# Where the first token tiles are loaded from in a layernorm prologue, and the order of its steps

## The chip, the cores and the metric

One core of a Trainium2 chip runs the kernel. The metric is the device time of one execution in microseconds (us). The kernel before takes 797.77 us, the median of three runs (797.47 to 797.81). Engines are named PE (TensorE), ACT (ScalarE), DVE (VectorE), POOL (GpSimd) and SP (SyncE, which computes nothing and issues transfers). ACT and SP both issue transfers here; such an issue is an instruction in the engine's own queue, which every engine works off in order.

## The reference

```
x  = A_x                      # 2048 tokens x 640, bf16
xn = layernorm(x)             # over the 640, no gain or bias
s  = softmax_attention(xn, wqkv) @ wo        # 32 heads of 20
g  = silu((sigmoid(xn @ w_gate) * (xn @ w_up)) @ w_down)   # 1728 wide
return x + s * g
```

## The kernel before

The 2048 tokens are 16 tiles of 128 tokens ("x0" to "x15"), each 128x640 bf16 or 160 KB. A prologue loads them, normalizes and transposes them, and computes keys, values and the first queries of the first heads. After it, a long main phase runs attention and the gated block, with its order written out by a planner at build time. The change touches the prologue alone.

**Loads.** Line 215 issues the 16 loads before any computing: x1 and x3 from ACT's queue, the other fourteen from SP's. Behind x7 come two loads of the first head group's weights (`wst`, line 127), behind x15 one load `wv` (line 139).

**Steps of a tile.** `s_stats` is mean and variance: on DVE two `bn_stats` and a `bn_aggr` (lines 270, 271), on ACT two activations with a sum (lines 275, 276; tiles 2, 5, 7, 11, 12 and 15). `s_rstd` on POOL (lines 280 to 285) takes two tiles at a time. Then `s_xn` on DVE (line 291), `s_tr` (five transposes on PE, line 298, into one of four `tp` buffers) and `s_ev` (copy out, DVE or ACT, line 301). For each chunk of four tiles follow `s_k` (key matmuls, line 318), `s_kt` (key copy, ACT, line 324), `s_kmax` (line 329); for the first chunks `s_v` and `s_vev` (values), and for the first `s_q`, `s_abs`, `s_bound`, `s_qev` (first queries). `s_table` is a tiny exponential (line 227 calls line 85) that brings in ACT's function table early.

**Order.** The steps form a graph of `Step` objects, each with an assumed duration per engine, an earliest time `at`, and a lateness weight (`L_...`, `EARLY`). A loop (lines 436 to 454) walks an assumed clock in steps of 0.02 us and gives each free engine the most urgent step that its assumed times allow; where PE has nothing it issues a `scrap` matmul on ones (line 451), so that PE stays busy. The loop only fixes the order in which instructions stand in each engine's queue. On the chip each waits for its real inputs. `X_AT` is the loop's assumed arrival of each x tile.

```
SP  L215 xt_114 (x7)
SP  L127 wst           waits DMAHW0   (x0)
SP  L127 wst           waits DMAHW1   (x1)
SP  L215 xt_115 (x8)   waits DMAHW2   (x2)
ACT L215 xt_108 (x1), xt_110 (x3)     no waits
```

## Time and profile before

| | |
|---|---|
| runs | 797.47, 797.77, 797.81 us |
| profiled execution | 797.83 us, of which the span of instructions is 795.6 us |
| granted clock | 0.999 |
| busy over the span | PE 97%, DVE 97%, ACT 98%, POOL 13% |
| first scores of the main phase (line 956) | start at 26.85 us |

Times in the text are microseconds from the start of the span. A row of the timeline gives start, duration, engine, line, operation, and in brackets the idle time of the engine before it with what ended it. "SPq" and "ACTq" are the transfer issues on those engines.

### The profile page before, as it was taken

The numbers are of one execution on the slowest core, as the hardware profiler recorded it, in microseconds if no ns is written. First come the engines' busy times: TensorE is split into PE (matmuls) and PEld (weight loads), VectorE is DVE, ScalarE is ACT, GpSimd is POOL, SyncE is SP. The second block draws the span as 40 slices with busy tenths as digits, with TensorE's granted clock in tenths as the row PEclk, the third lists the DMA queues.
The fourth block names the chain that finished last, engine by engine and source line by source line (L and its number), as shares of the span: only waits on it lengthen the run. The fifth ranks groups of instructions, "written<-read, shape, count | busy, mean of one in ns | idle before, by whom it ended". The sixth has DMA issues, their size and how long they took to land.

```text
span 795.6 us, 24034 instructions
## 1 busy us (share of the span) xinstructions
PE 771.1 (97%) x9799; PEld 264.0 (33%) x9803; DVE 770.0 (97%) x1243; ACT 779.6 (98%) x980; POOL 100.7 (13%) x200
## 2 busy tenths in 40 slices
PE   8999999999999999999999999999999999999997
PEld 6523222333233233333223332333333233332332
DVE  8899999999999999999999999999999989999997
ACT  8899999999999999999999999999999999999995
POOL 7100000000100001000010000000000000321421
PEclk9999999999999999999999999999999999999999
DMA  5632212223232133223133323233123222231221
GB/s 164 188 79 51 67 46 58 58 69 82 63 81 66 41 88 104 51 55 76 44 63 86 80 54 85 75 108 109 37 61 85 66 69 53 70 110 41 69 65 54
DMA packets 107461, 59.06 MB, mean 74 GB/s; under 512 B 53579, under 2 KB 102779, under 8 KB 107351
## 3 DMA queue, kind: packets, MB, share of 16 engines
q1 hardware_dynamic: 106647, 56.98, 27.8%
q8 instruction: 76, 1.25, 0.7%
q10 hardware_dynamic: 704, 0.56, 0.2%
q14 instruction: 34, 0.28, 0.1%
HBM read 43.21 MB, written 9.13 MB: 66 GB/s over the span
## 4 chain that ended last, share of the span: by engine, by line
ACT 56%; PE 21%; DVE 13%; issue 9%; DMA 1%; DVEq 0%; ACTq 0%
ACT pt L85 44%; PE bk L526 8%; PE scA L956 7%; ACT px L85 7%; DVE iv L1399 5%; PE oacc L993 4%; ACT tnh L85 4%; DVE pb L1101 2%; DVE pb L1095 1%; ACT td L85 1%; DVE pb L1098 1%; DVE stats L270 1%; DVE hT L743 1%; ACT aq L176 0%; DMA xt<-in_A_x_dram 0%
## 5 line engine op out<-in xcount | busy, mean ns | idle before, releaser
L85 ACT ACTIVATE pt<-scA 128x1024 bf16<-128x1024 f32 x707 | 699.9, 1172 | 0.4
L1399 DVE TENSOR_SCALAR iv<-bk 128x512 int16<-128x512 f32 x500 | 331.5, 680 | 10.2 <-PE bk L956 8.2
L956 PE MATMUL scA<-q,kT 32*128 32x512 bf16 x1407 | 274.9, 382 | 11.6 <-ACT pt L85 7.0
L956 PE MATMUL bk<-q,kT 32*128 32x512 bf16 x641 | 203.6, 383 | 0.2
L993 PE MATMUL oacc<-pt,v 128*21 128x512 bf16 x1407 | 185.4, 382 | 1.0 <-ACT pt L85 1.0
L956 PEld LDWEIGHTS <-kT 32*128 32x128 bf16 x2048 | 86.3, 91 | 287.4 <-issue 277.5
L993 PE MATMUL oacc<-pb,v 128*21 128x512 bf16 x1000 | 161.2, 382 | 0.1
L526 PE MATMUL bk<-xnT,wgu 128*32 128x512 bf16 x2160 | 159.2, 383 | 0.8
L1101 DVE TENSOR_TENSOR pb<-iv,pb 128x2048 bf16<-128x2048 bf16 (+1 forms) x126 | 152.7, 1212 | 0.8
L1049 POOL TENSOR_TENSOR on_bf<-on,rl 128x128 bf16<-128x128 f32 x116 | 56.4, 492 | 636.0 <-DVE pb L1101 186.1
L85 ACT ACTIVATE px<-bk 128x512 bf16<-128x512 f32 x141 | 102.6, 741 | 0.9 <-PE bk L956 0.9
L1095 DVE TENSOR_SCALAR pb<-iv 128x2048 int16<-128x2048 int16 (+1 forms) x126 | 85.8, 681 | 0.7
L1098 DVE TENSOR_SCALAR pb<-iv 128x2048 int16<-128x2048 int16 (+1 forms) x126 | 85.7, 680 | 0.0
L526 PE MATMUL bk<-hT,wd 128*32 128x512 bf16 x1120 | 82.6, 384 | 0.5 <-DVE hT L754 0.2
L993 PEld LDWEIGHTS <-v 128*21 128x21 bf16 x2548 | 52.6, 91 | 80.8 <-issue 58.8
L526 PEld LDWEIGHTS <-wgu 128*32 128x32 bf16 x2160 | 44.9, 95 | 62.0 <-issue 43.4
L526 PE MATMUL bk<-xnT,wu 128*32 128x512 bf16 x640 | 48.6, 383 | 0.2 <-DVE iv L1399 0.2
L993 PE MATMUL oacc<-px,v 128*21 128x512 bf16 x141 | 48.0, 382 | 0.0
L85 ACT ACTIVATE tnh<-bk 128x512 bf16<-128x512 f32 (+1 forms) x56 | 41.7, 745 | 0.1
L743 DVE SCALAR_TENSOR_TENSOR hT<-tnh,bk 128x512 bf16<-128x512 bf16 x52 | 35.3, 679 | 0.5 <-PE bk L526 0.2
L526 PEld LDWEIGHTS <-wd 128*32 128x32 bf16 x1120 | 20.5, 95 | 33.5 <-issue 27.1
L707 PE MATMUL bk<-wv,xnT 128*128 128x160 bf16 x280 | 28.0, 234 | 0.8 <-ACT px L85 0.6
(128 smaller groups left out, 397.4 us busy)
## 6 DMA issues: line engine op xcount, KB each, us to landing
rl<-rd SPq DMA_DIRECT2D x124, 64.0 KB
wgu<-in_B_w_gate_dram SPq DMA_DIRECT2D x24, 320.0 KB
wgu<-in_B_w_up_dram SPq DMA_DIRECT2D x24, 320.0 KB
xnT<-in_A_x_dram SPq DMA_DIRECT2D x16, 160.0 KB
xt<-in_A_x_dram SPq DMA_DIRECT2D x14, 160.0 KB
oU<-on_bf SPq DMA_DIRECT2D x108, 20.0 KB
wd<-in_B_w_down_dram SPq DMA_DIRECT2D x1, 2080.0 KB
out_dram<-xnT SPq DMA_DIRECT2D x13, 160.0 KB
```

What stands on the lines that cost most here:

```text
L85: return nc.scalar.add_instruction(mybir.InstActivation(func=func, name=nc.get_next_instruction_name(), engine=ENG.Activation, ins=[nc.sca ...
L270: nc.vector.bn_stats(out=stats[:, h, :], in_=xts[k][:, h * HD:(h + 1) * HD])
L526: nc.tensor.matmul(out[j:j + 32, :], lhsT=lhsT[:, j:j + 32], rhs=rhs, start=start, stop=stop, tile_position=(0, j), skip_group_check=True)
L707: nc.tensor.matmul(st["ps"][:, i * 2 * GC:(i + 1) * 2 * GC], lhsT=xn_tok(tts[i], kd), rhs=wvs[pr][:, kd, :], start=(kd == 0), stop=(kd == ...
L743: return nc.vector.scalar_tensor_tensor(out=hT[0:fs, kf, :], in0=st["t"][0:fs, :], scalar=1.0, in1=st["u"][0:fs, :], op0=ALU.add, op1=ALU. ...
L956: nc.tensor.matmul(dst, lhsT=kTs[gc_of(b)[0] % 2][32 * j:32 * j + 32, kt * P:(kt + 1) * P], rhs=qts[b % 3][32 * j:32 * j + 32, :], start=T ...
L993: nc.tensor.matmul(oacc[32 * j:32 * j + DH + 1, :], lhsT=lhsT, rhs=u["src"], start=first, stop=last, tile_position=(0, 32 * j), skip_group ...
L1049: ins = nc.gpsimd.tensor_tensor(out=on_bf[:, cs], in0=on[:, cs], in1=rl[:, cs], op=ALU.mult)
L1095: ins = nc.vector.tensor_scalar(out=pb[:, 0, :, :].bitcast(I16), in0=iv, scalar1=0x7F80, scalar2=1, op0=ALU.bitwise_and, op1=ALU.bitwise_or)
L1098: ins = nc.vector.tensor_scalar(out=pb[:, 1, :, :].bitcast(I16), in0=iv, scalar1=0x007F, scalar2=0x3F00, op0=ALU.bitwise_and, op1=ALU.bitw ...
L1101: ins = nc.vector.tensor_tensor(out=pb[:, 1, :, :], in0=iv.bitcast(BF16), in1=pb[:, 1, :, :], op=ALU.mult)
L1399: beat(nc.vector.tensor_scalar(out=d["iv"][:, j, :], in0=bank[bk], scalar1=B_OFF, scalar2=0.0, op0=ALU.add, op1=ALU.max))
```

## The change

x0, x1 and x2 now come from SP. The loads of x3 and x6 move to ACT, and no longer stand with the other loads: they are issued in the step `s_table`, behind the table load, and that step runs inside the loop, after all of SP's loads have been written down. In the loop `s_table` is allowed 2.9 us from 0.3. `X_AT` and several weights are new, which reorders some steps. No computation is added or taken out.

```diff
-    X_AT = (3.2, 3.4, 3.8, 4.3, 4.7, 5.2, 5.8, 6.4, 8.9, ...
+    X_AT = (3.2, 3.7, 4.2, 4.5, 4.8, 5.3, 5.5, 6.0, 8.4, ...
-    L_ST, L_CH, L_K, L_V, L_Q = 2.0, 1.5, 6.5, 9.5, 1.5
-    L_QH, L_QL, L_KT, L_KM, L_TR, L_EV = 14.5, 10.0, 2.0, 7.0, -4.0, 0.0
+    L_ST, L_CH, L_K, L_V, L_Q = 2.0, 1.5, 7.5, 9.5, 1.5
+    L_QH, L_QL, L_KT, L_KM, L_TR, L_EV = 14.5, 10.0, 2.0, 8.0, -8.0, 0.0
-    EARLY = {('stats', 14): 4.0, ('stats', 11): -2.0, ('ev', 9): -2.0, ('xn', 1): 8.0}
+    EARLY = {('stats', 14): 4.0, ('stats', 11): -2.0, ('xn', 1): 8.0, ('ev', 5): -2.0, ('xn', 15): 2.0, ('tr', 15): 8.0, ('tr', 9): 8.0}
+    ACT_LOADS = (3, 6)
...
         for k in range(TT):
-            (nc.scalar if k in (1, 3) else nc.sync).dma_start(out=xts[k], in_=x2[k * P:(k + 1) * P, :])
+            if k not in ACT_LOADS:
+                nc.sync.dma_start(out=xts[k], in_=x2[k * P:(k + 1) * P, :])
             if k == 7:
                 wst0 = load_wst(0)
         wv0 = load_wv(0)
...
         def s_table(eng):
             exp_act(eps_t, eps_t)
+            for k in ACT_LOADS:
+                nc.scalar.dma_start(out=xts[k], in_=x2[k * P:(k + 1) * P, :])
...
-        table = Step(s_table, (), {"ACT": 1.3}, at=1.3)
+        table = Step(s_table, (), {"ACT": 2.9}, at=0.3)
```

The built program of the changed kernel begins so on the two queues that issue transfers (line numbers are those of the changed file; the tile's number is added):

```
SP  L217 xt_107 (x0), xt_108 (x1), xt_109 (x2), xt_111 (x4), xt_112 (x5), xt_114 (x7)    no waits
SP  L127 wst, wst                                    no waits
SP  L217 xt_115 (x8)       waits DMAHW0
SP  L217 xt_116 (x9)       waits DMAHW1
SP  L217 xt_117 (x10)      waits DMAHW2
SP  L217 xt_118 (x11)      waits DMAHW3
...
ACT LoadActFuncSet
ACT L85  Activation eps_t
ACT L229 xt_110 (x3)       waits DMAHW0, until it has counted two transfers
ACT L229 xt_113 (x6)       waits DMAHW2, until it has counted two transfers
ACT L279 Activation sq (statistics of x2)
```

Past the prologue the order of instructions is the same on every engine. Within it, these steps stand elsewhere: on DVE the statistics of tile 14 ahead of those of tile 8, the `xn` of tile 15 ahead of the statistics of tile 13, `ev` of tile 15 ahead of the first `kmax`; on PE a scrap matmul between the transposes of tiles 7 and 10, the transposes of tile 15 ahead of those of tile 11, the last key matmuls of 256 columns into a `tp` buffer ahead of the transposes of tile 12; on ACT the first `abs` behind two copies, the second `kt` behind `ev` of tile 9, the narrow `kt` ahead of `ev` of tile 12. POOL's order is the same.

More of the change, by code (lines that the diff above doesn't have):

```diff
@@ L203 @@
     RH = 2
-    X_AT = (3.2, 3.4, 3.8, 4.3, 4.7, 5.2, 5.8, 6.4, 8.9, 9.4, 9.9, 10.4, 11.0, 11.5, 12.0, 12.6)
-    L_ST, L_CH, L_K, L_V, L_Q = 2.0, 1.5, 6.5, 9.5, 1.5
-    L_QH, L_QL, L_KT, L_KM, L_TR, L_EV = 14.5, 10.0, 2.0, 7.0, -4.0, 0.0
+    X_AT = (3.2, 3.7, 4.2, 4.5, 4.8, 5.3, 5.5, 6.0, 8.4, 8.9, 9.4, 9.9, 10.4, 10.9, 11.4, 12.0)
+    L_ST, L_CH, L_K, L_V, L_Q = 2.0, 1.5, 7.5, 9.5, 1.5
+    L_QH, L_QL, L_KT, L_KM, L_TR, L_EV = 14.5, 10.0, 2.0, 8.0, -8.0, 0.0
     KSB = (1, 1, 1, 0, 1)
-    EARLY = {('stats', 14): 4.0, ('stats', 11): -2.0, ('ev', 9): -2.0, ('xn', 1): 8.0}
+    EARLY = {('stats', 14): 4.0, ('stats', 11): -2.0, ('xn', 1): 8.0, ('ev', 5): -2.0, ('xn', 15): 2.0, ('tr', 15): 8.0, ('tr', 9): 8.0}
+    ACT_LOADS = (3, 6)
     ACT_STATS = (2, 5, 7, 11, 12, 15)
```

## The prediction

> **What bounds the kernel now.** First the page: three engines are nearly full, so time lost ahead of the main phase is not won back there.

> ```profile
> PE 771.1 (97%) x9799; PEld 264.0 (33%) x9803; DVE 770.0 (97%) x1243; ACT 779.6 (98%) x980; POOL 100.7 (13%) x200
> ```

> Then the chain of waits of the first 30 us, which opens with the load of x0 and runs on DVE:

> ```profile
> 0.80 3.03 DMA xt<-in_A_x_dram
> 3.86 0.90 DVE stats L270 x2
> 4.78 0.21 DVE mv L271
> 4.99 0.76 DVE stats L270 x2
> 5.77 0.21 DVE mv L271
> 5.98 0.76 DVE stats L270 x2
> ```

> Third, busy time by stretches. The columns are length, then PE, PEld, DVE, ACT, POOL:

> ```profile
> 4.00:10.00 6.00, 3.96 (x34) 2.84 (x32) 5.83 (x19) 5.19 (x13) 5.38 (x13) 1.00 0.97 289
> 10.00:16.00 6.00, 5.88 (x63) 4.63 (x62) 5.86 (x18) 5.90 (x14) 5.03 (x15) 1.00 0.60 145
> 16.00:22.00 6.00, 5.62 (x64) 4.19 (x63) 5.97 (x17) 5.95 (x13) 2.32 (x7) 1.00 0.00 1
> 22.00:25.00 3.00, 3.00 (x37) 2.53 (x36) 2.92 (x9) 2.07 (x4) 0.00 (x0) 1.00 0.00 0
> ```

> DVE is busy 20.58 of these 21 us: what delays it early in its queue delays the first scores (26.85) in full. Fourth, the timelines of the two issuing queues, ACT first:

> ```profile
> 0.80 0.88 ACTq L215 DMA_DIRECT2D xt<-in_A_x_dram  x2
> 1.71 1.28 ACT L85 ACT_TABLE_LOAD   x1 [1.71 <-PEq L1587]
> 4.72 0.74 ACT L275 ACTIVATE sq<-xt 128x640 bf16<-128x640 bf16 x1 [1.51 <-DMA xt<-in_A_x_dram]
> ```

> ```profile
> 0.80 2.80 SPq L215 DMA_DIRECT2D xt<-in_A_x_dram  x6
> 3.85 0.96 SPq L127 DMA_DIRECT2D wst<-in_A_wqkv_dram  x2
> 4.86 3.95 SPq L215 DMA_DIRECT2D xt<-in_A_x_dram  x8
> ```

> SP's first six issues end at 3.60, but the seventh starts only at 3.85, when x0 has landed (the trace has its semaphore full at 3.84). SP's waits name that gap:

> ```profile
> SPq L127 <- DMA xt<-in_A_x_dram: 0.2, 1, 0.2
> ```

> So the semaphore that a transfer shares with the one eight before it holds back its issue, and the queue behind it. That decides this change.

> **The waits that the change adds.** In program order x3 and x6 now come behind SP's loads. x3 shares its semaphore with x0 and x8 and is issued only when x8 has landed; x6 shares with x2 and x10 and waits for x10. Both waits stand on ACT ahead of its first statistics. Behind x3's issue are queued x6's issue, the statistics of x2, x5, x7 and all later ACT work; DVE's third item, the statistics of x3, waits for the landing. Before, x3 was issued at 1.23 and used at 5.90.

> **When x8 lands.** SP's issues take 2.80/6 = 0.467 us: x0, x1, x2, x4, x5, x7 from 0.80 to 3.60. The `wst` pair has fresh semaphores now and follows at once (0.96), so x8 is issued at 4.6; its own wait, for x0, is then over (x0 landed 3.03 after issue). From issue to landing: x0 3.03, x2 3.45 (1.27 to 4.72), x8 3.8 (4.86 to 8.65, by the trace's semaphores). The last had two more tiles ahead; landings of x5, x6 and x7 are 0.43 apart on average (6.37, 6.83, 7.23), so without them 3.8 - 0.86 = 2.9. I take 3.1, between the unloaded and the loaded rows: x8 lands at 7.7, ends 7.5 and 8.4.

> **When x3 lands.** Issued at 7.7. On ACT's queue x1 took 2.83 (0.80 to 3.63) and x3 3.28 (1.23 to 4.51). I take 2.9, nearer x1, since nothing stands ahead of it on its queue: 10.6, ends 10.3 and 11.85. DVE's statistics of x3 start at 10.6 instead of 5.90: **+4.7** (4.4 to 5.95).

> **ACT beside it.** x10 is issued two SP issues behind x8 (3.95/8 = 0.49 each, 0.55 behind the weights), about 5.7, and lands 3.2 later at 8.9. Then x6's issue (0.43) frees ACT at 9.35 instead of 4.72: +4.6. This lies beside DVE's +4.7; if x3 came early, ACT's delay would be the bound. x6 lands near 11.8, DVE wants it at 8.19 + 4.7 = 12.9: covered by 1.1, and past that it costs its lateness one for one.

> **x0, x1, x2 from SP.** x0 no longer shares its first microsecond with x1 and may land up to 0.4 earlier; that only moves DVE's statistics of x0 and x1 ahead of the new stall, so 0. x1 and x2, issued at 1.27 and 1.73, land by about 5 and are wanted at 4.9 and 9.35; a lateness of x1 falls into the same stall. The table load starts at about 0.85 instead of 1.71, hidden by the wait for x8: 0.

> **New order.** Instruction counts per engine are the same, so the price is only in waits. `xn` of tile 15 (0.39) ahead of the statistics of tile 13 delays POOL's `rstd` for tile 12 by 0.36 (it ended at 21.26, `xn` of tile 12 started at 21.36); `ev` of tile 15, moved ahead of `kmax`, delays that `xn` by 0.40 too, which keeps the cover at 0.1. The second `kt` goes behind a 0.58 copy, which puts its release of the key bank level with PE's next key matmuls. PE's transposes of tile 15, moved forward, have their `xn` some 0.5 earlier. Sum 0 to +0.2; I take 0. A gain is bounded by the whole slack of DVE, 21 - 20.58 = 0.4.

> **PE's rate after the stall.** PE ends its first 28 scraps at 6.43 and waits for the first `xn`, at 8.34:

> ```profile
> 1.31 5.12 PE L451 MATMUL scrap<-busy 128*128 128x256 bf16 x28 [1.31 <-DVE busy L430]
> 8.34 0.45 PE L298 MATMUL tp<-ident,xn 128*128 128x128 bf16 x5 [1.90 <-DVE xn L291]
> 8.62 0.93 PE L451 MATMUL scrap<-busy 128*128 128x256 bf16 x7
> ```

> 28 scraps in 5.12 us against 7 in 0.93: in the trace the first start 213 ns apart, those from 5.4 on 109 ns. PE started at half rate and took 3.9 us of work to leave it; 1.9 us of idling did not bring it back. (The page's clock column shows 1.00 throughout.) Now the first `xn` moves to 8.34 + 4.7 = 13.0, an idle of 6.6 us that no row has. The nearest rows are full rate after 1.9 idle and half rate at the start. I take half rate: 6.6 is over three times the idle shown harmless. Its cost: from the first transposes to `ev` of tile 3 on DVE, PE has 20 transposes of 55 ns and 8 scraps of 109 ns, 1.97 us, which become 3.94. Slack there is 0.41 idle ahead of 9.69, and 0.41 between the transposes of tile 3 (end 10.88) and DVE's `ev` (11.29). So +1.97 - 0.82 = **+1.2** (0 at full rate; 2.4 if it lasts into `q` and `k`, whose 1.2 us of doubling the later 0.34 idle hardly covers).

> [...]

> **Sum.** 4.7 + 0 + 1.2 = 5.9 on the profiled execution's 797.83 (span 795.6 and 2.2 around it; the median is 0.06 below): **803.7 us**. All later loads, the second `wst` too, move along with the work that frees their buffers.

> **Rivals.** (a) *The clock stays.* Everything as above with PE at full rate: 797.83 + 4.7 = 802.5. For it: 109 ns right after 1.9 us idle. Against: the start.

> (b) *Not slower: the issues do not wait.* If ACT sends both loads on at once, x3 goes out at 2.15 (0.85 + 1.28) and lands 2.9 later at 5.1, ahead of 5.90; x6 lands at 5.5, ahead of 8.19. Then only x0's up to 0.4 remains and DVE gains at most that: 797.4 to 797.8. It decides if x8 has landed by 5.9 - 2.9 = 3.0, or if the wait binds nobody. Against: x8 cannot be issued before 4.6, and SP's gap to 3.85 shows such a wait binding. It is also the case where the change does what its words say.

> [...]

> (c) *Longer.* x8 lands at 8.4, x3 takes 3.45, PE stays at half rate into `q` and `k`: 5.95 + 2.4 = 8.35, 806.2. For it: x8's 3.8 and x2's 3.45 before.

> **Numbers.** Forecast 0.60, (a) 0.22, (b) 0.06, (c) 0.12. The range leaves out (b) and most of (c): its low end is (a) with x3's early end, 797.83 + 4.4 = 802.2, less 0.4 for DVE's slack: 801.8. Its high end is x3's late end with +1.2, near 805.0, and 0.4 of the longer half rate: 805.4. A measurement of this kernel tells 0.2% (1.6 us) from no change. Faster by more: 0.01, (b) with a gain that its price doesn't hold; within: 0.05; slower: 0.94.

> **What would show it.** ACT's queue after: table load at 0.85, x3's issue near 7.7, x6's near 8.9, first statistics near 9.35. DVE: a second wait for a load, about 5 us, ended by x3 near 10.6. PE: scraps after 13.0 at 213 ns instead of 109. First scores near 32.7. It is wrong if x3's issue stands near 2.1, if DVE's wait is under 4 us, or if the first scores move by something other than DVE's wait plus PE's loss.

## The result, and the profile after

The changed kernel takes 806.02 us (median of 4 runs, 805.3 to 806.68); the kernel before, beside it, 797.79 (797.47 to 798.25). The ratio is 1.0103, 95% interval 1.0085 to 1.012: 8.2 us slower. The forecast was 803.7 with a range to 805.4, so the direction was right and the size too small.

The profiled execution took 805.3 us, its span 803.4 (before 795.6). The page's first section shows nearly the same busy time in a longer span:

```profile
PE 771.9 (96%) x9803; PEld 264.2 (33%) x9803; DVE 770.0 (96%) x1243; ACT 780.0 (97%) x980; POOL 99.6 (12%) x200
```

The chain of the first 37 us (start, length, what) now goes over SP's issues up to 4.66 and then over two transfers, one behind the other:

```profile
4.66 4.54 DMA xt<-in_A_x_dram
9.22 3.75 DMA xt<-in_A_x_dram
13.00 0.90 DVE stats L274 x2
...
15.48 0.71 PE tp L302 x5
16.20 1.49 PE scrap L455 x7
...
19.01 0.49 DVE xnT L305
...
34.60 0.39 PE scA L960 x2
```

The first is x8, from its issue to its landing, and the second x3. The first scores start at 34.60 instead of 26.85. That is +7.75, and the span grew by 7.8: all of the loss lies ahead of the main phase.

ACT's timeline shows the wait standing ahead of its first statistics:

```profile
0.80 1.28 ACT L85 ACT_TABLE_LOAD   x1 [0.80 <-PEq L1591]
9.22 1.16 ACTq L229 DMA_DIRECT2D xt<-in_A_x_dram  x2
10.42 0.74 ACT L279 ACTIVATE sq<-xt 128x640 bf16<-128x640 bf16 x1 [8.13 <-DMA xt<-in_A_x_dram]
```

SP's timeline has lost its gap ahead of the weights, and x8 goes out at 4.66 (4.86 before):

```profile
0.80 2.77 SPq L217 DMA_DIRECT2D xt<-in_A_x_dram  x6
3.62 1.00 SPq L127 DMA_DIRECT2D wst<-in_A_wqkv_dram  x2
4.66 4.45 SPq L217 DMA_DIRECT2D xt<-in_A_x_dram  x8
```

DVE's timeline: the first two tiles come early, then DVE idles 7.72 us for x3, whose statistics stood at 5.90 before.

```profile
3.15 0.89 DVE L274 BATCH_NORM_STATS2 stats<-xt 128x6 f32<-128x320 bf16 x2 [1.89 <-DMA xt<-in_A_x_dram]
4.20 0.83 DVE L274 BATCH_NORM_STATS2 stats<-xt 128x6 f32<-128x320 bf16 x2
13.00 0.89 DVE L274 BATCH_NORM_STATS2 stats<-xt 128x6 f32<-128x320 bf16 x2 [7.72 <-DMA xt<-in_A_x_dram]
```

Busy time by stretches (length, PE, PEld, DVE, ACT, POOL, then clock, DMA share and GB/s): DVE has 1.21 busy us of six in the first stretch, where it had 5.83.

```profile
4.00:10.00 6.00, 2.14 (x17) 1.54 (x15) 1.21 (x5) 0.00 (x0) 3.11 (x7) 1.00 0.91 264
10.00:16.00 6.00, 0.52 (x6) 0.52 (x7) 2.94 (x9) 5.03 (x12) 1.48 (x4) 0.62 0.51 151
```

PE's timeline: idle 9.35 us, then 7 scraps in 1.70 us where the same 7 took 0.93.

```profile
15.48 0.71 PE L302 MATMUL tp<-ident,xn 128*128 128x128 bf16 x5 [9.35 <-DVE xn L295]
15.99 1.70 PE L455 MATMUL scrap<-busy 128*128 128x256 bf16 x7
```

From these rows the loss splits in two. The statistics of x3 start at 13.00 instead of 5.90: **+7.1**. From there to the first scores it takes 21.60 us instead of 20.95: **+0.65**.

### The profile page after: what moved, and what is told of

It reads as the page before. It is cut to its first block, busy times and chain, and to the rows that moved or that the text cites. A ratio compares the mean times of both kernels' runs of the same rounds, so it can differ in the third digit from the quotient of the medians.

```text
span 803.4 us, 24037 instructions
## 1 busy us (share of the span) xinstructions
PE 771.9 (96%) x9803; PEld 264.2 (33%) x9803; DVE 770.0 (96%) x1243; ACT 780.0 (97%) x980; POOL 99.6 (12%) x200
## 4 chain that ended last, share of the span: by engine, by line
ACT 55%; PE 21%; DVE 13%; issue 9%; DMA 1%; SPq 0%; DVEq 0%; ACTq 0%
ACT pt L85 44%; PE bk L530 8%; ACT px L85 7%; PE scA L960 6%; DVE iv L1403 5%; PE oacc L997 4%; ACT tnh L85 4%; DVE pb L1105 2%; DVE pb L1099 1%; DVE pb L1102 1%; ACT td L85 1%; DMA xt<-in_A_x_dram 1%; DVE hT L747 1%; PE tp L302 1%; DVE stats L274 0%
## 5 line engine op out<-in xcount | busy, mean ns | idle before, releaser
L85 ACT ACTIVATE pt<-scA 128x1024 bf16<-128x1024 f32 x707 | 699.8, 1171 | 0.4
L1403 DVE TENSOR_SCALAR iv<-bk 128x512 int16<-128x512 f32 x500 | 331.2, 680 | 10.4 <-PE bk L960 8.5
L960 PE MATMUL scA<-q,kT 32*128 32x512 bf16 x1407 | 274.9, 382 | 11.5 <-ACT pt L85 7.0
L85 ACT ACTIVATE px<-bk 128x512 bf16<-128x512 f32 x141 | 102.6, 741 | 0.9 <-PE bk L960 0.9
L85 ACT ACTIVATE tnh<-bk 128x512 bf16<-128x512 f32 (+1 forms) x56 | 41.6, 743 | 0.1
L530 PEld LDWEIGHTS <-wd 128*32 128x32 bf16 x1120 | 20.5, 95 | 33.5 <-issue 27.1
```

What stands on the lines that cost most here:

```text
L85: return nc.scalar.add_instruction(mybir.InstActivation(func=func, name=nc.get_next_instruction_name(), engine=ENG.Activation, ins=[nc.sca ...
L530: nc.tensor.matmul(out[j:j + 32, :], lhsT=lhsT[:, j:j + 32], rhs=rhs, start=start, stop=stop, tile_position=(0, j), skip_group_check=True)
L960: nc.tensor.matmul(dst, lhsT=kTs[gc_of(b)[0] % 2][32 * j:32 * j + 32, kt * P:(kt + 1) * P], rhs=qts[b % 3][32 * j:32 * j + 32, :], start=T ...
L1403: beat(nc.vector.tensor_scalar(out=d["iv"][:, j, :], in0=bank[bk], scalar1=B_OFF, scalar2=0.0, op0=ALU.add, op1=ALU.max))
```

## The experiments

Theory A, which all the expectations start from: the late landing of x3 stops DVE, and it is late because its issue waits for the landing of x8; a smaller part is PE's half clock after the idle. The rivals put the cost on the block on ACT, on the new order of steps, or on the second queue. Later runs ask why the two landings came later than forecast. The diffs are against the changed kernel unless it says otherwise.

### The loads written at their place

x3 and x6 stay on ACT, behind an early table load, but stand among the other loads, so that their semaphores are fresh.

```diff
+        nc.vector.memset(eps_t, 0.0)
+        exp_act(eps_t, eps_t)
         for k in range(TT):
-            if k not in ACT_LOADS:
-                nc.sync.dma_start(out=xts[k], in_=x2[k * P:(k + 1) * P, :])
+            (nc.scalar if k in ACT_LOADS else nc.sync).dma_start(out=xts[k], in_=x2[k * P:(k + 1) * P, :])
...
         def s_table(eng):
-            exp_act(eps_t, eps_t)
-            for k in ACT_LOADS:
-                nc.scalar.dma_start(out=xts[k], in_=x2[k * P:(k + 1) * P, :])
+            pass
...
-        nc.vector.memset(eps_t, 0.0)
```

> The changed kernel with the loads of x3 and x6 written down at their place among the other loads (still ScalarE's queue, still behind the table load, new step order kept). The built program then gives neither a wait. Theory A (the issues wait for the landing of x8 and x10, eight transfers back on a shared semaphore): both go out by about 3 us, statistics of x3 start near 5.2 to 5.9, first scores near 26.9, total 797.6 to 798.2, ratio to before 1.000 +- 0.0006. Rival B (loads from ScalarE behind the table load are slow by themselves): x3 still lands several us later than 5.9, total above 801. Rival C (the new step order costs it): total near 806, since the order is kept.

Measured: 798.51 us (797.89 to 799.09, 10 runs), ratio to before 1.001 (1.0001 to 1.002). First scores at 27.6. ACT's timeline of this run:

```profile
0.80 1.28 ACT L85 ACT_TABLE_LOAD   x1 [0.80 <-PEq L1589]
0.97 0.86 ACTq L218 DMA_DIRECT2D xt<-in_A_x_dram  x2
5.29 0.74 ACT L278 ACTIVATE sq<-xt 128x640 bf16<-128x640 bf16 x1 [3.00 <-DMA xt<-in_A_x_dram]
```

Same queue, same transfers, same order of steps, only without the late partner to wait for: 7.3 of the 8.2 us are gone. The time is 0.3 above theory A's range, and 0.9 above the kernel before beside it (797.61). The chain of waits of this run goes over the landing of x5 and on over ACT's statistics:

```profile
3.23 4.06 DMA xt<-in_A_x_dram
7.32 0.84 ACT sq L278 x2
```

Before, x5's statistics started at 6.40. In this build one weight load also stands earlier, x8 is issued at 5.29 (4.86 before), and x2's statistics start at 5.29 (4.72 before). So the 0.9 goes with loads that land later on ACT's side; which part of the new distribution makes them later was not separated.

### The order alone, and the loads alone

First the kernel before with only `X_AT`, the weights and the table step's assumed time of the change; then the changed kernel with all of these put back.

> The kernel before with the new assumed arrivals, weights and step order, loads as before (x1 and x3 from ScalarE ahead of the table load). Theory A: the order by itself costs 0 to 0.2 us, total 797.6 to 798.1. Rival C: total 803 or more.

> The changed kernel's loads (x3 and x6 in the step with the table load) with the step order of before. Theory A: the same two waits, so the same delay as the changed kernel: statistics of x3 start at 12.5 to 13.5, first scores near 34.5, total 805 to 806.5. Rival C: total near 798.

Measured: order alone 797.54 (797.05 to 797.87, 10 runs), ratio 0.9998 (0.9988 to 1.0007), first scores at 27.0; loads alone 805.89 (805.14 to 806.1, 4 runs), ratio 1.0101 (1.0086 to 1.0116). The order costs nothing that can be measured, and the loads carry the whole loss. The chain of waits of the loads alone is a second sample of the same two transfers, x8 and x3: x8 takes less and x3 more, and the end (12.95) is the same to 0.02.

```profile
4.67 3.95 DMA xt<-in_A_x_dram
8.64 4.31 DMA xt<-in_A_x_dram
```

### The same late loads from SP

```diff
         wv0 = load_wv(0)
+        for k in ACT_LOADS:
+            nc.sync.dma_start(out=xts[k], in_=x2[k * P:(k + 1) * P, :])
...
-            for k in ACT_LOADS:
-                nc.scalar.dma_start(out=xts[k], in_=x2[k * P:(k + 1) * P, :])
```

> The changed kernel with the loads of x3 and x6 issued from SyncE, as the last behind x15 and wv, instead of from ScalarE; ScalarE's queue then holds no wait and does its statistics from about 4.7 on. x3 is issued near 9.7 (behind the landing of x9) and lands near 13.3 to 13.9. Theory A (the late data of x3 on VectorE sets the end, ScalarE's own blocked queue lies beside it): no gain, 806.0 to 807.0. Rival D (the blocked ScalarE queue is what costs): total 803 or less, although x3 is as late.

Measured: 806.44 (806.21 to 807.25, 4 runs), ratio 1.0108 (1.0091 to 1.0125). ACT starts its statistics at 4.73, nearly as before, and it brings nothing. SP's timeline of this run shows the two late issues:

```profile
9.16 1.00 SPq L222 DMA_DIRECT2D xt<-in_A_x_dram  x2
```

DVE's timeline shows that the statistics of x3 still wait for them:

```profile
13.14 0.89 DVE L274 BATCH_NORM_STATS2 stats<-xt 128x6 f32<-128x320 bf16 x2 [7.92 <-DMA xt<-in_A_x_dram]
```

The block on ACT is not the cost here; the late data are. Rival D falls.

### Only x3 at its place

x3 goes back among the loads as in the first experiment; x6 stays in `s_table`. In this build one weight load stands behind x2.

> Only x3 goes back to its place among the loads (from ACT's queue, behind an early table load; it waits for nothing). x6 stays in s_table, and its issue waits on ACT for the landing of x8, so ACT is still blocked. Theory A (DVE's wait for late data is the cost; ACT's block counts only once x3 is early): x8 is issued near 4.9 and lands 3.4 to 4.5 later, ACT is free near 9.0 to 9.9, x6 lands near 12 to 13.2. DVE has the statistics of x0, x1, x3, x4 early and then stops for x6 or for what ACT's statistics of x2 release: first scores 4 to 6 later than before, 802 to 804. Rival B (the block on ACT is covered by DVE's other work, only x3 counts): within 1.5 of 798.5. Rival C (ACT's block costs by itself as much as x3's lateness): 805 to 806.7, as the changed kernel.

Measured: 804.24 (six of 7 runs at 802.4 to 804.75, one at 811.32), ratio 1.0094 (1.0065 to 1.0122), the profiled run 802.4. The chain of waits of this run again has two transfers in a row, now x8 and x6, and DVE stops for x6:

```profile
4.71 3.78 DMA xt<-in_A_x_dram
8.51 3.86 DMA xt<-in_A_x_dram
12.39 0.90 DVE stats L276 x2
```

First scores at 31.8, 5.0 later than before; theory A's 4 to 6 holds in the profile, and the median is just past its 804. In the changed kernel x6's lateness was hidden behind x3's: x6 landed at 13.65 (by the trace's semaphores), and DVE came to its statistics only at 15.34. So both loads cost, but not in sum: mending one of them only shows the other.

### PE kept busy

Eighty more `scrap` matmuls on ones ahead of the first transposes, on PE alone.

```diff
+        for _ in range(80):
+            nc.tensor.matmul(scrap[:, 0:2 * P], lhsT=busy[:, 0:P], rhs=busy, start=True, stop=True)
```

> The changed kernel with 80 more scrap matmuls ahead of the first transposes, so that TensorE works until about 15 us instead of 6.13 and the first transposes (15.48) find it busy just before. Theory A with the clock as a part (TensorE idles 9.35 us in the changed kernel, falls to half rate, which costs 0.6 us between the statistics of x3 and the copy of tile 3 on VectorE: 6.01 us apart instead of 5.39 before): the two are 5.4 apart again, granted clock 1.00 from 13 to 19 us, total 0.6 us below the changed kernel, 805.0 to 805.8. Rival (the half rate is hidden, the 0.6 is something else): still 6.0 apart, total unchanged near 806.

Measured: 804.53 (804.4 to 805.38, 4 runs), ratio 1.0087 (1.0072 to 1.0102). The clock column stays at 1.00, and from the statistics of x3 (12.54) to the first scores (33.53) it takes 20.99 us, as before the change (20.95; 21.60 with the change). The 0.65 was the clock. The time fell by 1.5, more than the expected 0.6: x3 landed 0.46 earlier in this run's profile, and other runs of the changed kernel seem to have been longer at half clock than its profiled one (PE's clock, in the next section).

### Where the landings' time comes from

Four runs shift what is in flight beside the two transfers. First the weights (`wst`) behind x15:

> The changed kernel with the two loads of the first head group's weights (rows of 160 bytes) moved behind x15 on SyncE. x3 still waits for x8 and x6 for x10, but x8 is now issued near 3.6 instead of 4.66 and nothing with small rows lies ahead of it. In the changed kernel x8 took 4.56 us from issue to landing where 3.1 was forecast. Theory A1 (the small rows ahead made x8 late): x8 lands about 3.1 after issue, x3 is issued near 6.8 and its statistics start near 10.3, total 802.8 to 803.8. Rival A2 (one transfer engine among the sixteen happens to lag, whatever lies ahead): x8 takes 4 to 4.6 again, x3 is issued at 7.7 to 8.2, statistics of x3 near 11.7, total 804.2 to 805.2. Rival B and C: unchanged, near 806.

Then half the columns of the tiles ahead of x8 (x1, x2, x4, x5, x7), or of those behind it (x9 to x15). These kernels leave out part of the input: the other columns of these tiles are set to zero on DVE, further down in the edit.

```diff
+    HALF = (1, 2, 4, 5, 7)          # or range(9, TT)
...
-                nc.sync.dma_start(out=xts[k], in_=x2[k * P:(k + 1) * P, :])
+                w = HD if k in HALF else D
+                nc.sync.dma_start(out=xts[k][:, 0:w], in_=x2[k * P:(k + 1) * P, 0:w])
```

> The changed kernel, but of x1, x2, x4, x5 and x7 only the first 320 columns are loaded and the rest is set to zero by VectorE: half the bytes ahead of x8, as many transfers and rows. Part of the input is left out. In the changed kernel x8 took 4.56 us from issue to landing, with the small-row weights moved away 4.15. Theory A1 (bytes ahead on the same queue make x8 late): 3.0 to 3.4, x3 issued by 8.1. Rival A2 (the count of rows, or single transfer engines that lag): 3.8 to 4.6, x3 issued at 8.5 to 9.3. Total follows x3's issue one for one, 804.5 to 806.5.

> The changed kernel, but of x9 to x15 only the first 320 columns are loaded and the rest is set to zero by VectorE: half the bytes that run beside x3's load. Part of the input is left out. In the changed kernel x3 took 3.75 us from issue to landing, against 2.83 and 3.28 on the same queue before. Theory A3 (SyncE's loads beside it take the bandwidth): 2.8 to 3.3. Rival A4 (ScalarE's queue or single lagging transfer engines, whatever runs beside): 3.6 to 4.3. x8's landing should not move (9.2 +- 0.6). Total 804.8 to 806.5.

And both halves at once:

> The changed kernel with only the first 320 of 640 columns loaded of x1, x2, x4, x5, x7 and of x9 to x15 (the rest is set to zero): half the bytes ahead of x8 and half beside and behind it; x0, x3, x6 and x8 are whole. Theory A (both landings were forecast too early because the queued bytes of other loads stretch them; with less of them the forecast's own 3.1 and 2.9 come back): x8 lands 2.8 to 3.2 after its issue at 4.65, x3 is issued near 7.5 to 7.9 and lands 2.8 to 3.2 later, 10.4 to 11.0 (forecast 10.6). First scores 21.6 to 22.5 later, 32.0 to 33.5; time 802.9 to 804.3. Rival B (the two halves relieve the same thing, so that the second adds nothing to the first): x3 lands at 11.0 to 11.5, time 804.6 to 805.2.

All of it in one table, from the chains and timelines: from x8's issue to its landing, from x3's issue to its landing, start of DVE's statistics of x3, and the time with its ratio to before.

| kernel | x8 | x3 | stats x3 | time, ratio (interval) |
|---|---|---|---|---|
| forecast | 3.1 | 2.9 | 10.6 | 803.7 |
| changed | 4.54 | 3.75 | 13.00 | 806.02, 1.0103 (1.0085 to 1.012) |
| loads alone | 3.95 | 4.31 | 12.97 | 805.89, 1.0101 (1.0086 to 1.0116) |
| PE busy | 3.82 | 4.01 | 12.54 | 804.53, 1.0087 (1.0072 to 1.0102) |
| late loads from SP | 4.05 | 3.96 | 13.14 | 806.44, 1.0108 (1.0091 to 1.0125) |
| weights last | 4.13 | 3.71 | 11.50 | 804.44, 1.0083 (1.0068 to 1.0098) |
| half ahead | 3.36 | 4.64 | 12.71 | 805.53, 1.0097 (1.0077 to 1.0117) |
| half behind | 3.20 | 3.16 | 11.07 | 804.83, 1.0088 (1.0068 to 1.0109) |
| half of both | 2.76 | 3.48 | 10.96 | 803.88, 1.0079 (1.0061 to 1.0097) |

Each row but the forecast is one profile. Putting the weights last lets x8 out at 3.62 instead of 4.66, and that is its gain; the 4.13 lies within the 3.82 to 4.54 of the other runs with full loads, where A1 expected 3.1, so the small rows ahead were not what made x8 late. A2's numbers fit, but no run shows a single engine that lags. Half the bytes ahead take x8 to 3.36, as A1 expected; x3's 4.64 in that run, the longest of all, was not expected and stays open. Half the bytes *behind* take x8 to 3.20, although none of these was issued before it and the expectation had its landing unmoved, and they take x3, which is issued on another queue, to 3.16. So in these runs a landing depends on what is in flight beside it, issued before or after, on either queue. The two runs with less behind x8 also had fewer of the stalled packets that the last section shows, two and one against six to fourteen in the rows with full loads; for them the runs cannot tell fewer bytes from fewer stalls. x3 took 3.96 from SP's queue in one profile, and 3.75 to 4.31 from ACT's in the three others with the same loads: no difference between the queues shows here.

With both halves x3's statistics start at 10.96 (forecast 10.6) and the kernel takes 803.88: in time, the forecast described a queue with half the load, though x8 took less than its 3.1 and x3 more than its 2.9. x3's 3.48 is 0.3 over theory A's bound for its own part. In time and at x3's landing the run sides with theory A; x3 alone took a little longer than with the later half only, so the two halves do not simply add.

## Why the prediction was right or wrong

**The waits bind: right.** x3's issue stands right behind x8's landing (9.20 by the trace's semaphores, issue at 9.22); the trace has x0, x8 and x3 on one semaphore, with 16 counts each, the last at 3.12, 9.20 and 12.97. ACT's queue waits with it and DVE stops for x3. Rival (b) is out, and the first experiment shows that the partner alone makes the wait.

**When x8 lands: the first step that failed.** The forecast took x8's 3.8 of before, subtracted 0.86 for two tiles that no longer stood ahead, and settled on 3.1, with 3.8 as its late end. It measured 4.54, and 3.82 to 4.05 in the three other runs with the same loads up to there: the subtraction bought nothing. One of the two tiles was no load on x8 even before: x3 had landed at 4.51, and x8 went out at 4.86. The 3.8 was also a single sample; the order-only run, which has the loads of before, gives 4.13 (4.80 to 8.93, by the trace's semaphores). And the step priced only what stands ahead, while the seven tiles issued behind x8, the same before and after, weigh as much by the half-behind run. Why the absence of the other tile, x6, bought nothing either stays open. Term: +1.5.

**When x3 lands: the second.** The 2.9 came from x1, loaded at 0.80 with little in flight, with the reason that nothing stands ahead of x3 on ACT's queue. At 9.22 all seven tiles behind x8 were still in flight (they landed from 9.59 to 12.21), `wv` followed at 9.61, and x3 took 3.75 (3.71 to 4.64 in the runs with full loads behind it). Rival (c)'s 3.45 was too short as well. Term: +0.85. The two make 2.35 of the 2.4 by which DVE's stall, +7.1 instead of +4.7, was too small.

**ACT beside it: right in kind.** ACT was free at 10.42 (forecast 9.35), because x10 landed at 10.02 instead of 8.9, and it stayed beside the path. That x6 costs its lateness once it is no longer covered is what the run with only x3 at its place shows. The forecast also said that with x3 early ACT's delay would be the bound; this did not come about: in that run ACT began its statistics only at 8.92, but DVE stopped for x6's data.

**x0 to x2, the table, the order: right.** x0 lands 0.7 earlier (the forecast said at most 0.4), which only moves DVE's first two items ahead of the stall. The table load is hidden. The order alone is 0.9998 of before.

**PE's clock: right that it falls, and the size depends on the execution.** Half rate after the long idle was the forecast's estimate from two rows of before. The profile shows half clock and 0.65 instead of 1.2. The slack that the forecast took off was read a little too large: of its 0.41 ahead of 9.69, 0.11 is the last scrap's own time (it starts at 9.28), which leaves 0.30. In the loads-alone profile the same stretch (statistics of x3 to first scores) takes 22.13 us, +1.18. That profiled run took 806.1, the changed kernel's 805.3. The changed kernel's other runs have no trace, but their granted clock is on record: 0.993, 0.992 and 0.994, against 0.996 in the profiled one. Four profiles with 6.83 us of half clock show 0.995 to 0.996, four with 10.24 us show 0.992 to 0.993 (the last section has these lengths). So two of the three read like the longer half clock; the one at 0.994 lies between.

**Sum.** 7.1 + 0.65 = 7.75 against 4.7 + 1.2 = 5.9. With the longer half clock it is 7.1 + 1.18 = 8.3, near the 8.2 of the medians. Rival (c) came within 0.2 us of the median by luck, with another split: 5.95 of stall, which is too little, and 2.4 of clock, which is too much. The range ended too low because both its ends for the landings came from single rows of before, while four profiles of the same loads spread over 0.7 us for x8 and, on either queue, 0.6 for x3.

## What to carry to other kernels

Before moving a transfer in the program, count which one its semaphore is shared with: here a load moved from the fourth to the seventeenth place of the program waited for the ninth to land, and two transfers in a row stood on the path ahead of DVE where one, x0, had. Write a load that is needed early among the first ones, whatever queue issues it (798.51 us here with both loads in place on ACT's queue, 806.02 with them late there, 806.44 late on SP's). And price a transfer on a full queue with what is in flight beside it, behind it and on other queues too, and with the spread of several samples rather than one row: x8 took 3.20 us with half the bytes behind it, and 2.76 to 4.54 over the profiles here.

## What the runs showed of the hardware

**Half clock lasted 6.83 or 10.24 us.** PE's clock column in half-microsecond windows (length, busy PE, clock, DMA share, GB/s) places its fall and its return, of the changed kernel:

```profile
11.00:11.50 0.50, 0.00 (x0) 0.94 0.89 271
18.00:18.50 0.50, 0.50 (x9) 0.73 0.00 0
```

and of the loads alone:

```profile
9.00:9.50 0.50, 0.00 (x0) 0.93 0.91 236
19.50:20.00 0.50, 0.50 (x5) 0.83 1.15 185
```

The windows between read 0.50 in both, and so a value of 0.94 in a window of 0.5 us stands for half clock in its last 0.06 us. The clock fell at 11.44 and came back at 18.27 in the first, 9.43 and 19.67 in the second: 6.83 and 10.24 us. In all eight profiles in which it fell ahead of the main phase, the clock records show one of these two lengths. The fall came 5.3 us after the last scrap in the one and 2.6 in the other; with only x3 at its place it came 1.3 after (scraps to 9.43, fall at 10.73), sooner than the 1.9 of idling that the prediction read as harmless. So the length of the idle alone does not say when the clock falls, and what does was not shown. From the statistics of x3 to the first scores it took 0.65 longer than before in the changed kernel's profile, with 6.83 us of half clock, and 1.18 longer in the loads-alone one, with 10.24.

**Single packets stall.** In the packet records of the first 13 us a 1280-byte packet takes 0.055 us (median), but a few take 0.5 to 1.27. In the changed kernel one lasts from 7.67 to 8.81; the second weight load lands at 8.77, 1.77 behind the first, and x8 at 9.20, though the first of its 16 parts had landed at 7.46. Another, on ACT's queue, lasts from 11.55 to 12.27, ahead of x3's landing at 12.97. x3's issue at 9.22, which waited for x8, came behind the last of these parts and not the first, so one such packet may hold up a landing, and those behind. The records don't name the engine of a packet, so this link is by time alone, and why a packet stalls stays open. The half-ahead run had twelve such packets, the changed kernel six, half behind two, half of both one. Their count alone does not order the landings: loads alone had fourteen and PE busy twelve, and x8 came sooner there than in the changed kernel.

**An issue beside the table load.** In the first experiment ACT's queue issued two loads at 0.97, while the table load (0.80 to 2.08) was still running.
